# Attention and soft MoE on one core: key blocks of 128 within a batch, and value products over 128 rows

## The chip, the cores and the metric

The kernel runs on one core of a Trainium2 chip. The metric is device time in microseconds (us), from the first to the last instruction. An engine is named as in the profile: PE multiplies matrices (PEld loads its weights), DVE, ACT and POOL work on vectors, SP issues DMAs. [...]

## What is computed

Attention with one added to the denominator, over 8 batches, 12 heads, 448 positions and head size 64, and then a soft mixture of experts (32 slots, 8 experts) on the 3584 rows of 768.

```python
scores = scale * np.matmul(q, k.transpose(0, 1, 3, 2))
m = np.max(scores, axis=-1, keepdims=True)
e = np.exp(scores - m)
attn = e / (np.sum(e, axis=-1, keepdims=True) + np.exp(-m) + 1e-09)
x = np.matmul(attn, v)                       # then heads side by side: (3584, 768)
logits = x @ phi                             # softmax over rows gives slot inputs,
                                             # softmax over slots mixes the slot outputs
h = np.maximum(slot_input[e] @ w1[e], 0.0)   # per expert
slot_out[e] = h @ w2[e]
```

## The kernel before

**Units.** A unit u is two batches and two heads; 24 units run one after another, six (HP) to each pair of batches. A row of 448 positions is read as 64 partitions (P) of seven (TB) positions, so a tile has batch 0 in partitions 0 to 63 and batch 1 in 64 to 127, and seven blocks t of 64 positions per batch. C3 is 3: six of the seven query blocks are 128 wide, the seventh is 64 of each batch.

**Steps.** The program is a list of steps n, seven to a unit. In each step run, in this order, what the plan holds under "small", one score product (stage_S), what it holds under "mid" and "value", one transposed score product with its exp (stage_ST, 11 steps behind: LAG), and what it holds under "end" and "load". Every engine executes its instructions in the order in which this list issues them, and waits at the head of its queue. So a stage's place in a step is its place in every engine's queue.

**Stages of a unit that starts at step n = 7u.**
- load_qk (L114) and load_v (L120): q and k by DMA from POOL's queue with a cast to bf16, v by two DMAs from SP's queue in float32, after the cast of the v before it.
- stage_T (L194, step n - 1, mid): 28 transposes on PE into two banks; DVE copies the q half to SBUF (L204), ACT the k half (L205), behind it.
- stage_S (L208, steps n to n + 6): query x key scores, four products over a quarter of the array each; DVE reduces them to row maxima, a column of M (L219).
- stage_MT (L221, n + 7, small): PE transposes M, ACT copies it to mt (L225) and makes exp(-m), em (L227); POOL multiplies mt by a mask (L231, L237) into md.
- stage_ST (L242, n + 11 to n + 17): for key block t of 64 in both batches, ones x md subtracts the maximum and key x query adds the transposed scores; ACT writes exp of them to et (L256), four buffers.
- stage_V (L259, n + 10, load): POOL casts v to bf16 (L261) and sets a column of ones (L263).
- stage_AV (L266, steps n + AV0[t], mid): value products, et as weights; batch 0 over partitions 0 to 63 and batch 1 over 64 to 127, into a PSUM tile of two banks held from t = 0 until it is evacuated (16 products for each t).
- stage_AVout (L289, n + 19, value): ACT copies the tile to xu (L293) and xq (L296); xu is a single buffer.
- stage_shift (L300, n + 19, end): four small POOL copies bring the seventh block into place (L304); POOL adds em (L306) and 1e-9 (L307).
- stage_N (L310, n + 21, mid; n + 22, end, in units 1, 7, 13, 19): DVE's reciprocal (L313) and POOL's normalising product into x (L319).
- stage_X (L327, n + 27, value): PE transposes x, DVE copies it (L332).

After every sixth unit the mixture runs over the pair of batches, spread over the steps: logits, running maximum and sums over slots, gate softmax (L345 to L474). Weights come one load_w (L130) a unit on POOL's queue at step n + 7, "load", the rest after the last unit. Behind the steps come the experts' products and the output (L585 to L635).

**PSUM.** slot() (L94) hands out four buffers of two banks each, r0 to r3; each request takes the one that is due first by the LAGS table; the value products' buffer is out of the turn until release() (L101).

Of the kernel before, what the change touches and what calls it, by code (L numbers as in the profile page):

```python
# [9 lines left out]
F32 = mybir.dt.float32  # L10
# [6 lines left out]
P = 64  # L17
LAG = 11
AV0 = (15, 16, 16, 17, 18, 19, 19)
# [4 lines left out]
def kernel(  # L24
# [40 lines left out]
    for name, n, bufs in (("qr", N2, 1), ("kr", N2, 1), ("qk0", 2 * N2, 1), ("qk1", 2 * N2, 1),  # L65
                          ("vr", 2 * N2, 1), ("md0", N2, 1), ("v65", 2 * TB * 66, 1),
                          ("qk2", 2 * N2, 1), ("md1", N2, 1), ("v66", 2 * TB * 66, 1),
                          ("et", N2, 4), ("xu", 4 * TB * 65, 1), ("xq", 4 * 65, 1),
# [22 lines left out]
    LAGS = {"S": 3, "ST": 3.5, "T": 3, "X": 2.5, "M": 3, "held": 3.5}  # L91
    due, made, where = [0.0] * 4, [0], {}

    def slot(shape, dtype=F32, kind=None):  # L94
        made[0] += 1
        i = min(range(4), key=lambda j: (due[j], j))
        due[i] = made[0] + LAGS.get(kind, 2) if kind != "hold" else float("inf")
        where[kind] = i
        return psum.tile(shape, dtype, tag=f"r{i}", name="ps")

    def release():  # L101
        due[where["hold"]] = made[0] + LAGS["held"]

# [16 lines left out]
    def load_v(u):  # L120
        t_ = buf("vr", 0).bitcast(F32).rearrange("p (h n) -> p h n", h=2)
        RAW[u, "vr"] = load(u, t_, v, nc.sync if u else nc.gpsimd)
# [30 lines left out]
    ones = const.tile([128, P], BF16, name="ones")  # L153
# [8 lines left out]
    load_v(0)  # L162
    M = [const.tile([128, 128], BF16, name=f"m{i}") for i in range(2)]
# [27 lines left out]

    QT, KT, MD, ET, EM, AV, XU, X, DEN = {}, {}, {}, {}, {}, {}, {}, {}, {}

    def stage_T(u):  # L194
# [4 lines left out]
        for i, name in enumerate(("qr", "kr")):  # L199
            r = RAW.pop((u, name))  # L200
            for t in range(TB):
                for h in range(2):
                    nc.tensor.transpose(o[i][ds(h * D, D), :, ts(t, P)], r[:, h, ts(t, D)], ident)  # L203
# [4 lines left out]
    def stage_S(u, s):  # L208
        ps = slot([128, 2, 512], kind="S")
        for h in range(2):  # L210
            hs = ds(h * D, D)
            for r in range(2):

                b, o = divmod(s, C3) if s < 2 * C3 else (r, C3)
                o = o * 128 + (r * P if s < 2 * C3 else 0)
                nc.tensor.matmul(ps[ds(r * P, P), h, ds(0, S)], QT[u][hs, b, ds(o, P)],  # L216
# [4 lines left out]
    def stage_MT(u):  # L221
# [4 lines left out]
        em = small.tile([128, 2, TB], F32, tag="em", name="em")  # L226
# [15 lines left out]
    def stage_ST(u, t):  # L242
        ps = slot([128, 2, 512], kind="ST")
        for b in range(2):
            for h in range(2):
                hs = ds(h * D, D)
                nc.tensor.matmul(ps[ds(b * P, P), h, ds(0, S)], ones[hs, :], MD[u][hs, b, :],  # L247
                                 start=True, stop=False)
        for b in range(2):
            for h in range(2):  # L250
                hs = ds(h * D, D)
                nc.tensor.matmul(ps[ds(b * P, P), h, ds(0, S)],  # L252
                                 KT[u][hs, b, ds(t * P, P)], QT[u][hs, b, :],
# [5 lines left out]
    def stage_V(u):  # L259
# [3 lines left out]
        nc.gpsimd.memset(t_[:, :, :, ds(D, 1)], 1.0)  # L263
# [3 lines left out]

# [396 lines left out]
```

## Time and profile before

| what | value |
|---|---|
| runs | 356.85, 351.5, 354.83 us; median 354.83 |
| profiled execution | time and span 351.5 us |
| mean granted PE clock | 0.926 (1.00 in the main loop) |
| busy in the interval 69.64 to 79.49 us | PE 9.22, DVE 8.58, ACT 8.23, POOL 9.01 us |
| busy in 260.02 to 297.20 us (37.18 us) | PE 25.86, DVE 15.15, ACT 23.44, POOL 22.46 us |
| busy in 297.20 to 351.50 us (54.30 us) | PE 33.24, DVE 19.40, ACT 13.22, POOL 4.06 us |
| landing of a v load from SP | 3.2 to 10.6 us, median 7.2 |

The main loop runs from about 20 to 262 us; the last units, the experts and the output follow. A row of a timeline gives the start and the length of an instruction, or of several alike (xN), in us; in brackets stands how long its engine was idle ahead of it and which engine, tile and line ended that. Products on PE overlap, so their lengths do not add up; the distance between starts counts. Lengths on POOL are rough.

### The profile page before, as it was taken

The page shows a single profiled execution, that of the slowest core. Times are in us where ns is not written, and L with a number is a line of the kernel's source. Part 1 is how long each engine was busy: PE and PEld are TensorE (multiplying, and loading weights), DVE is VectorE, ACT ScalarE, POOL GpSimd, SP SyncE. Part 2 cuts the span into 40 slices and gives each one's busy share as a digit, 9 for nine tenths or more (in the row PEclk, how much of TensorE's full clock was granted, in tenths as well). Part 3 has the DMA queues.
Part 4 walks back from the last instruction along what each step waited for, and adds up shares of the span by engine and source line. Part 5 has one row for each costly group of instructions (what it writes and reads, how often), then busy time and mean ns, then how long its engine had stood idle before and what let it go on. Part 6 is the DMA issues. An engine that isn't in the chain of part 4 may idle for free.

```text
span 351.5 us, 14003 instructions
## 1 busy us (share of the span) xinstructions
PE 279.6 (80%) x6152; PEld 159.8 (45%) x6152; DVE 245.8 (70%) x321; ACT 223.1 (63%) x353; POOL 230.8 (66%) x413
## 2 busy tenths in 40 slices
PE   2679898998989789999968987899689745877760
PEld 1334554564555455556545544555455423342110
DVE  1886887988787978889888876878987015207440
ACT  1236887787778488888777776877588832015340
POOL 8335688899886878999876878698757573210000
PEclk9999999999999999999999999999999975596555
DMA  7455379789988898899997799869956599963997
GB/s 92 80 96 100 54 146 202 115 162 185 186 168 167 139 209 158 140 170 174 169 178 146 109 222 205 163 96 183 176 121 113 125 168 205 216 133 149 395 399 313
DMA packets 30061, 59.14 MB, mean 168 GB/s; under 512 B 4049, under 2 KB 22225, under 8 KB 30001
## 3 DMA queue, kind: packets, MB, share of 16 engines
q0 software_dynamic: 19344, 36.69, 61.7%
q1 hardware_dynamic: 10656, 21.57, 18.7%
q8 instruction: 48, 0.79, 0.9%
q14 instruction: 13, 0.10, 0.1%
HBM read 83.46 MB, written 11.01 MB: 269 GB/s over the span
## 4 chain that ended last, share of the span: by engine, by line
PE 31%; ACT 13%; DMA 12%; DVE 12%; issue 8%; POOL 6%; SPq 3%; ACTq 0%; POOLq 0%; DVEq 0%
PE ps L282 12%; ACT block L256 9%; PE ps L216 7%; DVE m L219 6%; PE ps L247 6%; DMA block<-in_moe_w_dram 5%; PE ps L252 4%; SPq L635 3%; DMA block<-in_v_dram 3%; DMA block<-in_k_dram 2%; DVE block L204 2%; DMA out_dram<-wres 2%; DVE sm L431 2%; ACT block L205 1%; POOL block L319 1%
## 5 line engine op out<-in xcount | busy, mean ns | idle before, releaser
L219 DVE TENSOR_REDUCE m<-ps 128x2 bf16<-128x896 f32 x168 | 179.5, 1090 | 41.4 <-PE ps L216 33.5
L256 ACT ACTIVATE block<-ps 128x896 bf16<-128x896 f32 x168 | 154.3, 922 | 49.9 <-PE ps L252 47.2
L216 PE MATMUL ps<-block 64*64 64x448 bf16 x672 | 66.6, 382 | 21.5 <-ACT block L205 12.0
L282 PE MATMUL ps<-block 64*128 64x65 bf16 (+1 forms) x2688 | 73.1, 196 | 4.2 <-issue 2.0
L282 PEld LDWEIGHTS <-block 64*128 64x128 bf16 (+1 forms) x2688 | 53.0, 97 | 42.6 <-issue 29.5
L247 PE MATMUL ps<-block,ones 64*64 64x448 bf16 x672 | 64.5, 364 | 5.4 <-ACT cT L445 2.4
L252 PE MATMUL ps<-block 64*64 64x448 bf16 x672 | 63.4, 356 | 0.0
L216 PEld LDWEIGHTS <-block 64*64 64x64 bf16 x672 | 32.3, 108 | 53.5 <-issue 37.4
L319 POOL TENSOR_TENSOR block<-block,rec 128x896 bf16<-128x896 f32 (+1 forms) x24 | 40.1, 1672 | 4.5 <-DVE rec L313 4.5
L304 POOL COPY block<-block 64x65 f32<-64x65 f32 x96 | 22.6, 236 | 26.5 <-ACT block L296 23.5
L231 POOL TENSOR_TENSOR block<-mt,nmask 128x768 bf16<-128x768 bf16 x24 | 36.0, 1502 | 3.9 <-ACT mt L225 2.7
L110 POOL DMA_DIRECT2D block<-in_q_dram x46 | 29.4, 640 | 14.0 <-PE ps L203 10.5
L205 ACT COPY block<-ps 128x896 bf16<-128x896 bf16 x24 | 21.8, 907 | 23.8 <-DVE block L204 23.8
L110 POOL DMA_DIRECT2D block<-in_k_dram x46 | 27.8, 618 | 2.0 <-issue 2.0
L247 PEld LDWEIGHTS <-ones 64*64 64x64 bf16 x672 | 23.5, 107 | 12.1 <-issue 7.4
L261 POOL CAST block<-block 128x896 bf16<-128x896 f32 x24 | 22.6, 941 | 5.8 <-DMA block<-in_v_dram 5.8
L203 PE MATMUL ps<-ident,block 128*64 128x128 bf16 x644 | 24.1, 228 | 2.0 <-DMA block<-in_q_dram 1.0
L203 PEld LDWEIGHTS <-block 128*64 128x64 bf16 x644 | 20.8, 115 | 8.2 <-issue 6.0
L252 PEld LDWEIGHTS <-block 64*64 64x64 bf16 x672 | 21.3, 109 | 0.9
L332 DVE COPY block<-ps 128x896 bf16<-128x896 bf16 x24 | 14.8, 616 | 9.7 <-PE ps L330 9.7
L293 ACT COPY block<-ps 128x780 f32<-128x780 f32 x24 | 19.5, 813 | 3.1 <-PE ps L282 2.0
L630 PE MATMUL ps<-wres,cT 32*128 32x384 bf16 x56 | 17.6, 493 | 4.5 <-DVE wres L633 2.5
(105 smaller groups left out, 254.4 us busy)
## 6 DMA issues: line engine op xcount, KB each, us to landing
wres<-in_moe_w_dram POOLq DMA_DIRECT2D x23, 768.0 KB, 7.7
out_dram<-wres SPq DMA_DIRECT2D x28, 384.0 KB, 4.2
block<-in_v_dram SPq DMA_DIRECT2D x46, 224.0 KB, 7.2
block<-in_moe_w_dram POOLq DMA_DIRECT2D x9, 768.0 KB, 12.8
block<-in_q_dram POOLq DMA_DIRECT2D x46, 112.0 KB, 4.8
block<-in_k_dram POOLq DMA_DIRECT2D x46, 112.0 KB, 4.5
block<-in_v_dram POOLq DMA_DIRECT2D x2, 224.0 KB, 4.2
wres<-in_q_dram POOLq DMA_DIRECT2D x2, 112.0 KB, 3.1
```

What stands on the lines that cost most here:

```text
L110: eng.dma_start(out=t_[ds(b * P, P), :, :], in_=src[bp * 2 + b, ds(hp * 2, 2)].rearrange("h (p t) d -> p h (t d)", t=TB))
L203: nc.tensor.transpose(o[i][ds(h * D, D), :, ts(t, P)], r[:, h, ts(t, D)], ident)
L205: nc.scalar.copy(t_[:, 1], o[1])
L216: nc.tensor.matmul(ps[ds(r * P, P), h, ds(0, S)], QT[u][hs, b, ds(o, P)], KT[u][hs, b, :], start=True, stop=True)
L219: nc.vector.tensor_reduce(m[:, :, s], ps[:, :, ds(0, S)], axis=AX.X, op=ALU.max)
L231: nc.gpsimd.tensor_tensor(md[:, :, ds(0, C3 * 128)].rearrange("p b (c n) -> p b c n", c=C3), mt.unsqueeze(1).unsqueeze(1).broadcast_to([12 ...
L247: nc.tensor.matmul(ps[ds(b * P, P), h, ds(0, S)], ones[hs, :], MD[u][hs, b, :], start=True, stop=False)
L252: nc.tensor.matmul(ps[ds(b * P, P), h, ds(0, S)], KT[u][hs, b, ds(t * P, P)], QT[u][hs, b, :], start=False, stop=True)
L256: nc.scalar.activation(et, ps[:, :, ds(0, S)], AF.Exp, scale=scale)
L261: nc.gpsimd.tensor_copy(t_[:, :, :, ds(0, D)], RAW.pop((u, "vr")).rearrange("p h (t d) -> p h t d", t=TB))
L282: nc.tensor.matmul(o, et[bs, h, ds(c * 128, w)], V65[u][bs, h, t, ds(0, 65)], start=(t == 0 and h == 0 and c == 0), stop=(t == TB - 1), sk ...
L319: eng.tensor_tensor(xo[:, hs], xv[:, hs, :, ds(0, D)], rec[:, hs].unsqueeze(3).broadcast_to([128, nh, TB, D]), op=ALU.mult)
```

## The change

Keys are put in another order by the k transposes (KPOS), so that 128 consecutive columns of K hold blocks c and c + 4 of one batch, and the last 64 hold block 3. v is loaded in the same order, by four DMAs in place of two. A key step then covers 128 keys of one batch (three steps for each batch) and one step 64 keys of both. The value products of a batch go over 128 rows into one bank of their own; batch 0 is evacuated at step n + 18, batch 1 at n + 21, by one ACT copy each. The shift moves to n + 21 and the normalising to n + 23 (n + 24 in units 1, 7, 13, 19), now in three POOL operations. Scores of a 128-wide query block are one product for each head in place of two. PSUM has three buffers of two banks and two of one bank, which also serve small tiles. em gets three buffers. The column of ones in v is set once at the start, on DVE. Three late weight loads move by one or two steps.

```diff
-AV0 = (15, 16, 16, 17, 18, 19, 19)
+AV0 = (15, 15, 17, 17, 19, 19, 20)
+AVO = (18, 21)
...
-    LAGS = {"S": 3, "ST": 3.5, "T": 3, "X": 2.5, "M": 3, "held": 3.5}
-    due, made, where = [0.0] * 4, [0], {}
+    LAGS = {"S": 3, "ST": 3.5, "T": 3, "X": 2.5, "M": 3}
+    due = {f"r{i}": 0.0 for i in range(3)} | {f"a{i}": 0.0 for i in range(2)}
+    made, held = [0], []
 
     def slot(shape, dtype=F32, kind=None):
         made[0] += 1
-        i = min(range(4), key=lambda j: (due[j], j))
-        due[i] = made[0] + LAGS.get(kind, 2) if kind != "hold" else float("inf")
-        where[kind] = i
-        return psum.tile(shape, dtype, tag=f"r{i}", name="ps")
+        one = mybir.dt.size(dtype) * shape[1] * (shape[2] if len(shape) > 2 else 1) <= 2048
+        small_ = [i for i in ("a0", "a1") if one and (kind == "AV" or due[i] <= made[0] + 1)]
+        i = min(small_ or ("r0", "r1", "r2"), key=lambda j: (due[j], j))
+        if kind == "AV":
+            assert due[i] < float("inf")
+            held.append(i)
+            due[i] = float("inf")
+        else:
+            due[i] = made[0] + LAGS.get(kind, 2)
+        return psum.tile(shape, dtype, tag=i, name="ps")
...
     def load_v(u):
         t_ = buf("vr", 0).bitcast(F32).rearrange("p (h n) -> p h n", h=2)
-        RAW[u, "vr"] = load(u, t_, v, nc.sync if u else nc.gpsimd)
+        bp, hp = divmod(u, HP)
+        for b in range(2):
+            src = v[bp * 2 + b, ds(hp * 2, 2)].rearrange("h (p t) d -> p h (t d)", t=TB)
+            for r, t0, t1, at_ in ((0, 0, C3 + 1 - b, b * (C3 + 1)), (1, C3 + 1 - b, TB, b * C3)):
+                (nc.sync if u else nc.gpsimd).dma_start(
+                    out=t_[ds(r * P, P), :, ds(at_ * D, (t1 - t0) * D)],
+                    in_=src[:, :, ds(t0 * D, (t1 - t0) * D)])
+        RAW[u, "vr"] = t_
...
+    for i in range(2):
+        nc.vector.memset(buf(f"v6{5 + i}", 0).rearrange("p (n e) -> p n e", e=66)[:, :, ds(D, 1)], 1.0)
...
+    KPOS = (0, 2, 4, 6, 1, 3, 5)
...
-                    nc.tensor.transpose(o[i][ds(h * D, D), :, ts(t, P)], r[:, h, ts(t, D)], ident)
+                    nc.tensor.transpose(o[i][ds(h * D, D), :, ts(KPOS[t] if i else t, P)],
+                                        r[:, h, ts(t, D)], ident)
...
-            for r in range(2):
-
-                b, o = divmod(s, C3) if s < 2 * C3 else (r, C3)
-                o = o * 128 + (r * P if s < 2 * C3 else 0)
-                nc.tensor.matmul(ps[ds(r * P, P), h, ds(0, S)], QT[u][hs, b, ds(o, P)],
+            if s < 2 * C3:
+                b, c = divmod(s, C3)
+                nc.tensor.matmul(ps[:, h, ds(0, S)], QT[u][hs, b, ts(c, 128)],
+                                 KT[u][hs, b, :], start=True, stop=True)
+                continue
...
     def stage_ST(u, t):
         ps = slot([128, 2, 512], kind="ST")
-        for b in range(2):
+        b, c = divmod(t, C3 + 1)
+        blocks = [(b, slice(0, 128), ts(c, 128))] if t != C3 else [
+            (b, ds(b * P, P), ds(C3 * 128, P)) for b in range(2)]
+        for b, rows, ks in blocks:
             for h in range(2):
                 hs = ds(h * D, D)
...
-        nc.gpsimd.memset(t_[:, :, :, ds(D, 1)], 1.0)
...
+            et = ET[u, t]
+            bs = (0, 1) if t == C3 else (t // (C3 + 1),)
+            if part == 0 and t in (0, C3):
+                AV[u, bs[-1]] = slot([128, 512], kind="AV")
             for h in range(2):
                 for c in (range(C3) if part == 0 else (C3,)):
-                    for b in range(2):
-                        bs = ds(b * P, P)
+                    for b in bs:
+                        av = AV[u, b]
+                        ks = ds(b * P, P) if t == C3 else slice(0, 128)
...
-                        nc.tensor.matmul(o, et[bs, h, ds(c * 128, w)],
-                                         V65[u][bs, h, t, ds(0, 65)],
+                        nc.tensor.matmul(o, et[ks, h, ds(c * 128, w)],
+                                         V65[u][ks, h, t, ds(0, 65)],
...
+    def stage_AVout(u, b):
+        xu = buf("xu", 0).bitcast(F32).rearrange("p (b n) -> p b n", b=2)
+        nc.scalar.copy(xu[:, b], AV.pop((u, b))[:, ds(0, TB * 65)])
+        XU[u] = xu.rearrange("p b (s e) -> p b s e", e=65)
         release()
 
     def stage_shift(u):
-        xu, xq = XU[u]
-        for h in range(2):
-            for b in range(2):
-                nc.gpsimd.tensor_copy(xu[ds(b * P, P), h, TB - 1, :], xq[ds(h * P, P), b, :])
+        xu = XU[u]
+        xq = buf("xq", 0).bitcast(F32)
+        R = 2 * C3
+        nc.gpsimd.tensor_copy(xq[ds(0, P)], xu[ds(P, P), 0, R])
+        nc.gpsimd.tensor_copy(xu[ds(P, P), 0, R], xu[ds(0, P), 1, R])
+        nc.gpsimd.tensor_copy(xu[ds(0, P), 1, R], xq[ds(0, P)])
         den = small.tile([128, 2, TB], F32, tag="den", name="den")
-        nc.gpsimd.tensor_tensor(den, xu[:, :, :, D], EM.pop(u), op=ALU.add)
+        em = EM.pop(u)
+        nc.gpsimd.tensor_tensor(
+            den[:, :, ds(0, R)].rearrange("p b (h c) -> p b h c", h=2),
+            xu[:, :, ds(0, R), D].rearrange("p b (h c) -> p b h c", h=2),
+            em[:, :, ds(0, R)].rearrange("p h (b c) -> p b h c", b=2), op=ALU.add)
+        nc.gpsimd.tensor_tensor(den[:, :, R], xu[:, :, R, D], em[:, :, R], op=ALU.add)
         nc.gpsimd.tensor_scalar(den, den, 1e-9, None, op0=ALU.add)
...
     def stage_N(u):
-        xv = XU.pop(u)[0]
+        xv = XU.pop(u)
+        R = 2 * C3
...
+        for b in range(2):
+            eng = nc.vector if b and u == U - 1 else nc.gpsimd
             eng.tensor_tensor(
...
+                x[:, ts(b, C3)].rearrange("p c (h d) -> p h c d", h=2),
+                xv[:, b, ds(0, R), ds(0, D)].rearrange("p (h c) d -> p h c d", h=2),
...
+        nc.gpsimd.tensor_tensor(
+            x[:, R].rearrange("p (h d) -> p h d", h=2), xv[:, :, R, ds(0, D)],
+            rec[:, :, R].unsqueeze(2).broadcast_to([128, 2, D]), op=ALU.mult)
...
-        at(n + 19, "value", lambda u=u: stage_AVout(u))
-        at(n + 19, "end", lambda u=u: stage_shift(u))
-
-        at(n + (22 if u % HP == 1 else 21), "end" if u % HP == 1 else "mid",
+        for b in range(2):
+            at(n + AVO[b], "value", lambda u=u, b=b: stage_AVout(u, b))
+        at(n + AVO[1], "end", lambda u=u: stage_shift(u))
+        at(n + AVO[1] + (3 if u % HP == 1 else 2), "end" if u % HP == 1 else "mid",
            lambda u=u: stage_N(u))
```

## The prediction

> **What bounds the kernel now.** I read the page's busy times first, then the stretches by stage, then the timeline of each engine over one period of the main loop, and the chain of waits last. The page shows four engines that are nearly equally loaded, so no share of busy time says which one counts:
>
> ```profile
> PE 279.6 (80%) x6152; PEld 159.8 (45%) x6152; DVE 245.8 (70%) x321; ACT 223.1 (63%) x353; POOL 230.8 (66%) x413
> ```
>
> The main loop makes one unit (two batches, two heads) per seven steps n; I call n mod 7 the phase. I cut it at the start of the copy of K (L205), which runs once per unit. The 20 intervals from 38.9 to 260.0 us last 9.85 us at best. Here is one of them, 69.64 to 79.49, on DVE, ACT, POOL and PE (timeline; columns: start, length, engine, line, operation):
>
> ```profile
> 68.99 0.61 DVE L204 COPY block<-ps 128x896 bf16<-128x896 bf16 x1
> ...
> 71.09 1.10 DVE L219 TENSOR_REDUCE m<-ps 128x2 bf16<-128x896 f32 x1 [0.96 <-PE ps L216]
> 72.10 0.23 DVE L313 RECIPROCAL rec<-den 128x14 f32<-128x14 f32 x1
> 72.25 6.69 DVE L219 TENSOR_REDUCE m<-ps 128x2 bf16<-128x896 f32 x6
> ```
>
> DVE never pauses except 0.96 us behind the K copy: seven maxima, two copies and a reciprocal are the interval. Delay one maximum and the interval grows by as much.
>
> ```profile
> 69.64 0.91 ACT L205 COPY block<-ps 128x896 bf16<-128x896 bf16 x1 [0.37 <-DVE block L204]
> ...
> 71.25 0.27 ACT L225 COPY mt<-ps 128x128 bf16<-128x128 bf16 x1
> ...
> 74.15 1.97 ACT L256 ACTIVATE block<-ps 128x896 bf16<-128x896 f32 x2 [0.31 <-PE ps L252]
> 76.44 0.92 ACT L256 ACTIVATE block<-ps 128x896 bf16<-128x896 f32 x1 [0.32 <-PE ps L252]
> 77.32 0.81 ACT L293 COPY block<-ps 128x780 f32<-128x780 f32 x1
> ...
> 79.49 0.91 ACT L205 COPY block<-ps 128x896 bf16<-128x896 bf16 x1 [0.37 <-DVE block L204]
> ```
>
> The exp of phase 4 starts at 76.44 (6.80 us into the interval) and ends at 77.36. The next line of PE that matters is the score product of phase 6:
>
> ```profile
> 68.81 0.56 PE L330 MATMUL ps<-ident,block 128*128 128x128 bf16 x7
> ...
> 74.21 0.51 PE L282 MATMUL ps<-block 64*128 64x65 bf16 x16
> 74.54 0.36 PE L247 MATMUL ps<-block,ones 64*64 64x448 bf16 x4
> ...
> 77.43 0.36 PE L216 MATMUL ps<-block 64*64 64x448 bf16 x4
> ```
>
> It starts 0.07 us after that exp: following slot() through the steps, the scores of phase 6 get the PSUM slot that the exp of phase 4 has just read. From the end of that exp to the next K copy are 79.49 - 77.36 = 2.13 us: product, last maximum, copy of Q, copy of K.
>
> ```profile
> 70.43 1.28 POOL L110 DMA_DIRECT2D block<-in_q_dram  x2 [0.21 <-issue]
> 71.70 1.21 POOL L110 DMA_DIRECT2D block<-in_k_dram  x2
> 72.89 1.51 POOL L231 TENSOR_TENSOR block<-mt,nmask 128x768 bf16<-128x768 bf16 x1
> 74.32 0.44 POOL L237 TENSOR_TENSOR block<-mt,nmask 128x128 bf16<-128x128 bf16 x1
> 74.68 1.72 POOL L319 TENSOR_TENSOR block<-block,rec 128x896 bf16<-128x896 f32 x1
> 76.31 0.62 POOL L141 DMA_DIRECT2D wres<-in_moe_w_dram  x1
> ...
> 78.36 1.06 POOL L304 COPY block<-block 64x65 f32<-64x65 f32 x4 [0.27 <-ACT block L296]
> 79.51 0.21 POOL L306 TENSOR_TENSOR den<-block,em 128x14 f32<-128x14 f32 x1
> 79.82 0.26 POOL L307 TENSOR_SCALAR den<-den 128x14 f32<-128x14 f32 x1
> ```
>
> POOL is full too, but its order suits the others: shift (phase 5), loads of Q and K, mask products, normalising (phase 0). L319 ends at 76.40 and ACT overwrites its input xu (L293) only at 77.32. That cover of 0.92 us is what the change touches.
>
> **The change, part by part.**
>
> *Scores and transposed scores (PE).* Six of seven steps lose half their products (12 and 24 per unit). A group of four quarter-array products takes 0.19 us (L247 at 73.49, L252 at 73.68), the time of its 448 columns; two half-array products have the same columns. I take 0; the bounds are 0 and +0.19 us per group if the two halves did not overlap (the pairs in L282 do).
>
> *Value products (PE).* 112 per unit become 48 over 128 rows and 16 over 64. 16 now take 0.33 us (74.21 to 74.54), 41 ns a pair; 56 pairs become 48 + 8 = 56 turns of the array. If a turn costs a pair, the change is 0, and I take that. Bounds: 65 columns at 448 per 0.19 us are 28 ns, 56 x (28 - 41) = -0.7 us per unit; the seven full-array transposes L330 take 0.51 us from 68.81 to the next group, 73 ns each, 48 x (73 - 41) = +1.5 us. Nearest is the pair, with the same 65 columns. One step with value products fewer saves one switch of array shape. [...]
>
> *Evacuation (ACT).* One copy of 780 (813 ns) and one of 130 (272 ns) become two of 455. The line through both rows, 0.83 ns an element, gives 543 ns each; back to back the old pair took 0.87 us (77.32 to 78.19), the new ones about 0.45 each. Cost 0 to +0.1. They move to phases 4 and 0, ahead of the exp there.
>
> *Shift (POOL).* Four copies at 0.265 become three; one add becomes two (0.31 each with its gap): 1.72 becomes 1.76 us. It moves from phase 5 to the end of phase 0, behind the mask products and past the loads of Q and K.
>
> *Normalising (POOL).* Rows 128x896 at 1704 ns and 128x448 at 956 give 1.67 ns an element: two of 384 and one of 128 are 0.77 + 0.77 + 0.34 = 1.88 us with overlapped issue, against 1.63 now. It moves from phase 0 to phase 2, behind the shift and the weight load (0.62). In units 1, 7, 13, 19 it comes one step later still. The memset L263 goes (0.16; two go to DVE at the start), off the path.
>
> *Loads of V (SP, DMA).* Two become four, of the same bytes in pieces of 768 and 1024 B. SP, otherwise idle here, takes about 0.6 us for each: +1.2. Landing is 7.2 us in the median, 10.6 at most; between one cast and the next lie 9.85 - 0.95 = 8.9 us. I take 0 while the interval is 11 us or more; bounds 0 and a landing twice as long if the four wait for each other.
>
> *PSUM.* The seven-step order of big slots stays: three of two banks for S, ST and T where four were shared with AV. The transposed maxima, X and the small tiles of the mixture use the two one-bank slots. 0, or a small gain where a score product had waited for the maxima's slot (interval 59.33 to 69.64: the first maximum waits 1.40 us).
>
> *What ends last then.* Time from the K copy: maxima copied on ACT at 1.88 (71.52). Loads of Q and K, now straight after PE's transposes (68.81), are issued by then. Mask products 1.93 to 3.72 (72.89 to 74.68 now is 1.79). Shift to 5.48. Weight load to 6.13. Normalising to 8.01. The reciprocal on DVE waits for the shift till 5.5, where the third maximum ends at about 4.9; the maxima queued behind it are 0.8 us late. But the evacuation of phase 4 overwrites xu, and must wait for all three parts of the normalising: 8.1. Behind it on ACT waits the exp: 8.55 to 9.47. Behind that the scores of phase 6, and 2.13 us later the K copy: **11.6 us** in place of 9.85. The 0.8 us are inside this, not added.
>
> The 14 intervals without mixture work sum to 145.7 us (9.84, 10.59, 10.31, 9.85, 10.78, 10.17, 10.82, 9.86, 9.85, 9.86, 10.82, 12.18, 9.87, 10.9); what lengthens some lies beside the new chain, so 14 x 11.6 = 162.4: +16.7. One has two weight loads: +0.6. Three with the gate's sums (13.6) normalise after the fourth maximum: 122.05 + 1.9, against an exp at 122.78 that now starts at 124.5: +1.7 each, +5.1. Three with logits (11.5 to 11.8): between 0 and 1.75, half of it: +2.6. At the end POOL's cast of unit 22 comes at 8.95 in place of 7.6 after the copy, then two more issues on SP, then 0.25 of normalising: +2.8. Sum +27.8 on the profiled execution's 351.5: **379**. That execution is the lowest of the three runs, whose median is 3.3 above; I say **380**.
>
> **Rivals.**
> 1. *The chain binds in part* (its rows on POOL are rough, and ACT comes later than reckoned). With 0.7 us an interval for 1.7, 351.5 + 20 x 0.7 + 2.8 = 368; with 0.2, 358. Against: every link is an in-order queue.
> 2. *Full-array products bind PE.* PE is busy 9.22 of 9.85 us; +1.5 and the 0.54 idle behind the K copy make 11.3. Alone: 14 x 11.3 - 145.7 + 6 x 1.45 = +21, 373; under the chain, nothing. [...]
> 3. *V late.* Four loads in a row on SP that wait for each other: 14 us to land, the cast pushes all POOL: 3 us an interval, 410. Partly so: 390 to 400. For: DMA engines are busy 0.91 of this interval. Against: only two waits for V now (5.8 us).
> 4. *Faster: fewer PE instructions.* 6152 products become about 4140. Four intervals hold a pause of about 0.9 us inside L282 with "issue" as its cause (86.35, 30 of 32 products, then 0.73 idle). Were these gone, and the waits on the maxima's slot, all 14 would be 9.85: -7.8, 344. It decides only if the normalising ends by 6.3 us into the interval, 1.7 before my sum: the shift would have to be ahead of the mask products on POOL, and its place in the step says it isn't.
>
> **How the numbers follow.** Chain as summed 0.56 (own range 369 to 391); in part 0.16; PE 0.08; V late 0.08; faster or no change 0.12. About 2% (7 us) is what a measurement of this kernel can tell from no change. Faster by more than that: 0.07, the better half of rival 4. Within it: 0.12, the rest of rival 4 and the lowest of rival 1. Slower: 0.81. The range 359 to 398 leaves out rival 4, and the worst of rival 3.
>
> **What would show it.** Right: intervals between K copies of 11.3 to 12 us; the evacuation of batch 0 on ACT idle till POOL's last normalising part; DVE idle ahead of the reciprocal, and ahead of the seventh maximum; the value products at about 41 ns a turn; POOL's order as listed. Wrong: intervals under 10.5 us, or ACT reaching that copy after POOL is done. A gap of PE between 128-row products would be rival 2; POOL's cast waiting for V rival 3.

## The result, and the profile after the change

| | before | after |
|---|---|---|
| median, us (before: all runs, those beside the new kernel too) | 354.6 | 396.63 (393.91 to 399.22) |
| ratio to before, 95% interval | | 1.122 [1.112, 1.132] |
| profiled span, us | 351.5 | 397.4 |
| regular interval between K copies, us | 9.85 | 11.90 |

The change made the kernel slower by 12%, and the chain that was predicted binds. The result is inside the predicted range (359 to 398), but at its upper end: the chain as summed had a range of 369 to 391 of its own, and 396.6 lies above it. Only the room that the range left for a late v takes it in. On the profiled executions the change costs 45.9 us where the sum said 27.8 (42.0 by the medians; the profiled execution after is the longest of its four). The part on why the prediction was right is about that difference. A span is 1.7 to 2.2 us less than the time wherever the record has both, so the kernel before's lowest time and its profiled execution, both 351.5, may be two executions. Single executions more than 1.5% above the fastest of the same kernel are left out of all ratios and of the medians of the experiments.

In the new kernel the K copy is L224, exp L279, evacuation L312, mask products L252 and L258, shift L320 to L330, reciprocal L337, normalising L341 and L346, POOL's cast of v L284, score products L233 and L237, maxima L240, transposed scores L271 and L276, value products L303. The page's first part and four of its groups of instructions:

```profile
PE 300.5 (76%) x4136; PEld 158.7 (40%) x4136; DVE 249.5 (63%) x323; ACT 220.7 (56%) x353; POOL 233.9 (59%) x438
...
L224 ACT COPY block<-ps 128x896 bf16<-128x896 bf16 x24 | 21.7, 905 | 44.2 <-DVE block L223 44.2
...
L341 POOL TENSOR_TENSOR block<-block,rec 128x384 bf16<-128x384 f32 x47 | 38.1, 836 | 5.6 <-DVE rec L337 5.3
L312 ACT COPY block<-ps 128x455 f32<-128x455 f32 x48 | 25.9, 543 | 21.0 <-POOL block L346 21.0
...
L337 DVE RECIPROCAL rec<-den 128x14 f32<-128x14 f32 x24 | 5.7, 238 | 23.6 <-POOL den L330 23.6
```

A third of PE's instructions are gone, and every engine but PE has almost the busy time it had; PE's rose from 279.6 to 300.5 us. What is new stands in the last column: ACT's evacuation waits 21.0 us for POOL's last normalising part (18 waits), DVE's reciprocal 23.6 us for the shift. Here is one regular interval, 76.88 to 88.78; first ACT and POOL in the timeline:

```profile
76.88 0.91 ACT L224 COPY block<-ps 128x896 bf16<-128x896 bf16 x1 [1.55 <-DVE block L223]
...
79.17 2.86 ACT L279 ACTIVATE block<-ps 128x896 bf16<-128x896 f32 x3
83.06 0.92 ACT L279 ACTIVATE block<-ps 128x896 bf16<-128x896 f32 x1 [1.04 <-PE ps L276]
85.07 0.54 ACT L312 COPY block<-ps 128x455 f32<-128x455 f32 x1 [1.09 <-POOL block L346]
85.50 1.73 ACT L279 ACTIVATE block<-ps 128x896 bf16<-128x896 f32 x2
88.78 0.91 ACT L224 COPY block<-ps 128x896 bf16<-128x896 bf16 x1 [1.54 <-DVE block L223]
```

```profile
78.85 1.46 POOL L252 TENSOR_TENSOR block<-mt,nmask 128x768 bf16<-128x768 bf16 x1 [0.32 <-ACT mt L246]
80.39 0.40 POOL L258 TENSOR_TENSOR block<-mt,nmask 128x128 bf16<-128x128 bf16 x1
80.85 0.23 POOL L320 COPY block<-block 64x65 f32<-64x65 f32 x1
...
82.09 0.25 POOL L330 TENSOR_SCALAR den<-den 128x14 f32<-128x14 f32 x1
82.40 0.64 POOL L156 DMA_DIRECT2D wres<-in_moe_w_dram  x1
83.06 1.63 POOL L341 TENSOR_TENSOR block<-block,rec 128x384 bf16<-128x384 f32 x2
84.63 0.40 POOL L346 TENSOR_TENSOR block<-block,rec 128x128 bf16<-128x128 f32 x1
```

POOL runs without a gap from the mask products (1.97 us after the K copy) to the end of the normalising (85.03, 8.15 after it). The evacuation starts 0.04 us later, after 1.09 us of idle time, and the exp queued behind it starts at 85.50. Then DVE and PE:

```profile
80.58 1.10 DVE L240 TENSOR_REDUCE m<-ps 128x2 bf16<-128x896 f32 x1 [0.17 <-PE ps L233]
82.37 0.24 DVE L337 RECIPROCAL rec<-den 128x14 f32<-128x14 f32 x1 [0.70 <-POOL den L330]
82.53 3.02 DVE L240 TENSOR_REDUCE m<-ps 128x2 bf16<-128x896 f32 x3
86.91 1.10 DVE L240 TENSOR_REDUCE m<-ps 128x2 bf16<-128x896 f32 x1 [1.36 <-PE ps L237]
```

```profile
78.96 0.72 PE L303 MATMUL ps<-block 128*128 128x65 bf16 x16
79.61 0.36 PE L271 MATMUL ps<-block,ones 64*128 64x448 bf16 x2
...
86.48 0.38 PE L237 MATMUL ps<-block 64*64 64x448 bf16 x4 [0.95 <-ACT block L279]
86.80 0.50 PE L303 MATMUL ps<-block 128*128 128x65 bf16 x8
87.13 0.95 PE L221 MATMUL ps<-ident,block 128*64 128x128 bf16 x28
```

The seventh score product starts at 86.48, as the first of the two exps ends (85.50 and 0.92 for one), and the last maximum waits 1.36 us for it. Sixteen 128-row value products take 79.61 - 78.96 = 0.65 us: 41 ns a turn, the pace of the pairs before.

### The profile page after: what moved, and what is told of

It is laid out like the page before. It is cut to its first block, busy times and chain, and to the rows that moved or that the text cites. A ratio compares the mean times of both kernels' runs of the same rounds, so it can differ in the third digit from the quotient of the medians.

```text
span 397.4 us, 10049 instructions
## 1 busy us (share of the span) xinstructions
PE 300.5 (76%) x4136; PEld 158.7 (40%) x4136; DVE 249.5 (63%) x323; ACT 220.7 (56%) x353; POOL 233.9 (59%) x438
## 3 DMA queue, kind: packets, MB, share of 16 engines
HBM read 83.46 MB, written 11.01 MB: 238 GB/s over the span
## 4 chain that ended last, share of the span: by engine, by line
POOL 26%; PE 20%; DMA 19%; ACT 11%; DVE 11%; issue 10%; SPq 1%; POOLq 0%; ACTq 0%; DVEq 0%
DMA block<-in_v_dram 9%; ACT block L279 8%; POOL block L341 5%; POOL block L252 5%; PE ps L303 5%; DMA block<-in_moe_w_dram 5%; PE ps L221 4%; DMA out_dram<-wres 4%; DVE m L240 4%; DVE block L223 3%; PE ps L271 2%; POOL block L118 2%; PE ps L233 2%; PE ps L237 2%; POOL wres L156 2%
## 5 line engine op out<-in xcount | busy, mean ns | idle before, releaser
L240 DVE TENSOR_REDUCE m<-ps 128x2 bf16<-128x896 f32 x168 | 178.9, 1090 | 67.4 <-PE ps L233 44.3
L279 ACT ACTIVATE block<-ps 128x896 bf16<-128x896 f32 x168 | 152.2, 924 | 58.8 <-PE ps L276 56.6
L233 PE MATMUL ps<-block 64*128 64x448 bf16 x288 | 57.3, 393 | 25.3 <-ACT block L279 9.3
L303 PE MATMUL ps<-block 128*128 128x65 bf16 (+3 forms) x1536 | 73.5, 203 | 3.8 <-POOL block L284 1.7
L271 PE MATMUL ps<-block,ones 64*128 64x448 bf16 (+1 forms) x384 | 65.5, 386 | 12.2 <-DVE m L240 10.6
L303 PEld LDWEIGHTS <-block 128*128 128x128 bf16 (+3 forms) x1536 | 54.8, 102 | 35.6 <-issue 22.1
L276 PE MATMUL ps<-block 64*128 64x448 bf16 (+1 forms) x384 | 64.0, 375 | 0.0
L233 PEld LDWEIGHTS <-block 64*128 64x128 bf16 x288 | 22.4, 99 | 70.1 <-issue 60.6
L224 ACT COPY block<-ps 128x896 bf16<-128x896 bf16 x24 | 21.7, 905 | 44.2 <-DVE block L223 44.2
L252 POOL TENSOR_TENSOR block<-mt,nmask 128x768 bf16<-128x768 bf16 x24 | 35.3, 1471 | 16.9 <-ACT mt L246 16.8
L341 POOL TENSOR_TENSOR block<-block,rec 128x384 bf16<-128x384 f32 x47 | 38.1, 836 | 5.6 <-DVE rec L337 5.3
L312 ACT COPY block<-ps 128x455 f32<-128x455 f32 x48 | 25.9, 543 | 21.0 <-POOL block L346 21.0
L271 PEld LDWEIGHTS <-ones 64*128 64x128 bf16 (+1 forms) x384 | 18.7, 98 | 35.7 <-DVE m L240 15.4
L284 POOL CAST block<-block 128x896 bf16<-128x896 f32 x24 | 22.3, 928 | 7.9 <-DMA block<-in_v_dram 7.9
L337 DVE RECIPROCAL rec<-den 128x14 f32<-128x14 f32 x24 | 5.7, 238 | 23.6 <-POOL den L330 23.6
L660 DVE COPY wres<-ps 128x768 f32<-128x768 f32 x14 | 13.4, 958 | 10.3 <-DMA out_dram<-wres 8.6
```

Of the source, the lines that this page charges most:

```text
L233: nc.tensor.matmul(ps[:, h, ds(0, S)], QT[u][hs, b, ts(c, 128)], KT[u][hs, b, :], start=True, stop=True)
L240: nc.vector.tensor_reduce(m[:, :, s], ps[:, :, ds(0, S)], axis=AX.X, op=ALU.max)
L252: nc.gpsimd.tensor_tensor(md[:, :, ds(0, C3 * 128)].rearrange("p b (c n) -> p b c n", c=C3), mt.unsqueeze(1).unsqueeze(1).broadcast_to([12 ...
L271: nc.tensor.matmul(ps[rows, h, ds(0, S)], ones[hs, ds(0, P * 2 // len(blocks))], MD[u][hs, b, :], start=True, stop=False)
L276: nc.tensor.matmul(ps[rows, h, ds(0, S)], KT[u][hs, b, ks], QT[u][hs, b, :], start=False, stop=True)
L279: nc.scalar.activation(et, ps[:, :, ds(0, S)], AF.Exp, scale=scale)
```

## The experiments

Ratios are to the kernel before, in runs made together with it. "Interval" is the regular distance between K copies in the profiled execution. A forecast's total is a time, to be held against the median.

| run | made from | median, us | ratio [95%] | span, us | interval, us |
|---|---|---|---|---|---|
| e1_xu2 | after | 386.2 | 1.086 [1.077, 1.095] | 381.2 | 10.89 |
| e2_order | after | 400.5 | 1.127 [1.119, 1.134] | 399.9 | 12.13 |
| e4_vr2 | after | 396.2 | 1.114 [1.106, 1.122] | 394.7 | 11.90 |
| e8_xu2_order_vr2 | after | 369.2 | 1.037 [1.031, 1.043] | 367.8 | 10.89 |
| e10_spread | e8 | 360.7 | 1.013 [1.007, 1.019] | 356.5 | 10.50 |
| e3_oldplace | after | 371.6 | 1.047 [1.040, 1.053] | 368.7 | 10.16 |
| e6_old_vr2 | e3 | 360.9 | 1.014 [1.008, 1.019] | 359.3 | 10.16 |
| e5_moved | before | 373.3 | 1.047 [1.039, 1.054] | 374.2 | 10.46 |
| e5b_moved | before | 358.8 | 1.011 [1.007, 1.016] | 356.1 | 10.46 |
| e9_v4 | before | 367.5 | 1.032 [1.025, 1.039] | 364.7 | 9.85 |
| e11_tsep | e6 | 353.6 | 0.996 [0.993, 0.999] | 351.3 | 10.45 |
| e12_tsep_x | e11 | 347.3 | 0.981 [0.975, 0.987] | 345.5 | 9.94 |

### Is it the single xu buffer? e1_xu2

```diff
-        xu = buf("xu", 0).bitcast(F32).rearrange("p (b n) -> p b n", b=2)
+        xu = wres[:, WRES - 1, ds(0, 4 * TB * 65)] if u % 2 and u < 20 else buf("xu", 0)
+        xu = xu.bitcast(F32).rearrange("p (b n) -> p b n", b=2)
```

> The changed kernel with a second buffer for xu (units with odd numbers up to 19), nothing else. Theory (the evacuation of batch 0 on ACT waits for the normalising on POOL): that wait goes, the interval between K copies falls from 11.9 us to what DVE's wait for the shift leaves, about 9.85 + 0.85 = 10.7 us, in some 16 intervals; total 397 - 19 = 375 to 382 us. Rival (128-row value products or the three two-bank PSUM buffers hold the loop): no change, 393 to 399. Rival (v in four pieces, two landings one behind the other): no change, or POOL's cast now waits for v and the interval stays above 11.

Measured: interval 10.89, the ratio down from 1.122 to 1.086. ACT's timeline, 71.98 being a K copy:

```profile
78.16 0.92 ACT L279 ACTIVATE block<-ps 128x896 bf16<-128x896 f32 x1 [1.04 <-PE ps L276]
78.98 0.53 ACT L313 COPY block<-ps 128x455 f32<-128x455 f32 x1
79.39 0.94 ACT L279 ACTIVATE block<-ps 128x896 bf16<-128x896 f32 x1
```

The evacuation follows the exp without a pause, and the interval loses 1.01 us: the predicted wait was the end of the chain. The total misses its forecast (386.2 for 375 to 382). In the profiled execution one interval is 17.15 us, with a POOL cast waiting 5.4 us for v, and the next 14.11. DVE's reciprocal still waits 0.71 us for the shift there (77.48), and I took that for what holds 10.89.

### The shift ahead of the mask products: e2_order, then e8_xu2_order_vr2

```diff
         EM[u] = em
+        MT[u] = mt
+
+    def stage_MD(u):
+        mt = MT.pop(u)
...
         at(n + 7, "small", lambda u=u: stage_MT(u))
+        at(n + 7, "end", lambda u=u: stage_MD(u))
```

The mask products, now a stage of their own, stand in POOL's queue behind the shift of two units before.

> The changed kernel with POOL's mask products issued behind the shift instead of ahead of it. Theory (xu's wait binds, DVE's wait for the reciprocal lies inside it): the reciprocal no longer waits, but the normalising ends no earlier, since the same operations lie ahead of it and the shift waits for the evacuation of batch 1 at 2.4 us: interval 12.2 us, total 397 to 405. Rival (DVE's wait for the shift binds): 0.85 us less in 20 intervals, 380. Rival (PE or PSUM): no change, 393 to 399.

As expected: the reciprocal does not wait, but the normalising comes no sooner, the evacuation waits 27.1 us for it in place of 21.0, and the interval is 12.13. In e8 the same edit stands with the second xu buffer, and with a second buffer for raw v (e4's edit, below).

> The changed kernel, its places kept, with the three waits taken away: a second buffer for xu, a second buffer for raw v (both for odd units up to 19), and the mask products issued behind the shift so that DVE's reciprocal does not wait. Theory: the interval falls from 11.9 to 10.0 to 10.4 us; the units from 20 on, with single buffers, stay slow; total 358 to 368. If each of the two waits could hold the loop alone, the second buffer of xu (10.9) and the order (12.1) show it only together. Rival (PE or PSUM): 378 or more.

The forecast was missed (interval 10.0 to 10.4, total 358 to 368). The interval did not move from 10.89, though the wait on the reciprocal was gone from it (in DVE's timeline it starts at 78.50, with no idle time ahead). So that wait had cost nothing, and my reading of e1 was wrong. PE's timeline, 73.80 being a K copy, shows what ends last:

```profile
78.15 0.36 PE L236 MATMUL ps<-block 64*128 64x448 bf16 x2 [0.22 <-ACT block L286]
78.45 0.95 PE L310 MATMUL ps<-block 128*128 128x65 bf16 x24
79.33 0.36 PE L278 MATMUL ps<-block,ones 64*128 64x448 bf16 x2
...
80.95 0.36 PE L236 MATMUL ps<-block 64*128 64x448 bf16 x2 [0.50 <-ACT block L286]
81.25 0.72 PE L310 MATMUL ps<-block 128*128 128x65 bf16 x16
```

The score product of phase 3 waits for an exp to free its PSUM slot (PSUM holds the tiles `ps`, which PE writes). Behind it stand 24 value products (0.88 us), then the transposed scores and their exp (79.98), then the next score product at 80.95, 7.15 us after the K copy, again behind an exp. In e1 it is 79.13 - 71.98 = 7.15 too.

The span fell by 13.4 us even so. The two late intervals that were 17.15 and 14.11 in e1 are 10.90 and 11.66, and the three with the gate's sums are 12.4 where they were 14.5 to 15.8. In those, one DVE instruction had taken 2.38 us while POOL ran its mask product; here the product comes later, and it takes 0.24 (last section).

### The value products spread as before: e10_spread

```diff
-AV0 = (15, 15, 17, 17, 19, 19, 20)
+AV0 = (15, 16, 16, 17, 18, 19, 19)
```

> The run e8_xu2_order_vr2 with the value products spread over steps as before (AV0 = 15, 16, 16, 17, 18, 19, 19). Theory (the 10.9 us left in e8 come from PE, where the value products of two key steps stand in one step ahead of the transposed scores): the interval falls to 10.1 to 10.4, total 355 to 361. Rival (the evacuation in phase 0 and 4 on ACT is what holds 10.9): no change, 367 to 371.

10.50 (0.1 above the forecast) and a total of 360.7: the lumped value products ahead of the transposed scores cost 0.4 us an interval. The span falls by 11.3, of which 6.4 lie in the 14 ordinary intervals, the rest ahead of them, in those with mixture work and behind the last.

### All places as before the change: e3_oldplace, e6_old_vr2

```diff
-AV0 = (15, 15, 17, 17, 19, 19, 20)
-AVO = (18, 21)
+AV0 = (15, 16, 16, 17, 18, 19, 19)
+AVO = (19, 19)
...
-        at(n + AVO[1] + (3 if u % HP == 1 else 2), "end" if u % HP == 1 else "mid",
+        at(n + (22 if u % HP == 1 else 21), "end" if u % HP == 1 else "mid",
```

> The changed kernel with the places of before: value products in steps 15 to 19, both evacuations at 19, shift at 19, normalising at 21 or 22. Key blocks of 128, products over 128 rows, five PSUM buffers and four v loads stay. Theory (the cost is the place on POOL's and ACT's queues): intervals of 9.9 to 10.3 us, total 350 to 362, where two landings of v one behind the other (about 9 us) may just hold POOL's cast. Rivals (PE, PSUM): still 380 or more. Rival (v): POOL's cast waits in most units, 370 or more.

The interval fell to 10.16, but the total by less than expected, which spoke for the rival on v. The waits of POOL:

```profile
POOL block L284 <- DMA block<-in_v_dram: 27.3, 9, 7.8
```

Nine casts wait for v, 27.3 us in all. e6 adds the second raw buffer of v, loaded a unit earlier:

```diff
+        t_ = wres[:, WRES - 2, ds(0, 2 * N2)] if u % 2 and u < 20 else buf("vr", 0)
...
+        if u + 2 < 21:
+            at(n + 10, "load", lambda u=u: load_v(u + 2))
```

> The changed kernel with the places of before and a second buffer for raw v (odd units up to 19). Theory (what was left of the loss with the old places was v's four loads, which land in two turns): POOL's cast no longer waits, intervals of 10.0 to 10.2 us, total 352 to 360. Rival (128-row products and three PSUM buffers cost as well): 364 or more.

Between the two forecasts. By the medians, e3 is 16.9 us over before, and 10.7 of them were the loads of v (371.6 to 360.9). The rest does not lie in the ordinary intervals, although the regular one is 10.16 against 9.85: the 14 sum to 145.5 us in e6 and to 145.7 before, where several were longer than regular. Of the 7.8 us that e6's span has more, 3.5 are in the three intervals with the gate's sums, 1.4 in those with logits, 1.1 ahead of the fourth K copy and 2.0 behind the last. With its stages in their old places the changed tiling costs 1.4%, and with e3's loads of v 4.7%. The places cost most of the 12%: 1.122 against 1.047 with one buffer for v, 1.114 (e4, below) against 1.014 with two.

### The loads of v alone: e9_v4, e4_vr2

e9 is the kernel before, with its two loads of v cut in four:

```diff
-        RAW[u, "vr"] = load(u, t_, v, nc.sync if u else nc.gpsimd)
...
+        for t0, t1 in ((0, C3 + 1), (C3 + 1, TB)):
+            for b in range(2):
+                src = v[bp * 2 + b, ds(hp * 2, 2)].rearrange("h (p t) d -> p h (t d)", t=TB)
+                (nc.sync if u else nc.gpsimd).dma_start(
+                    out=t_[ds(b * P, P), :, ds(t0 * D, (t1 - t0) * D)],
+                    in_=src[:, :, ds(t0 * D, (t1 - t0) * D)])
...
```

> The kernel before with the load of v cut into four pieces of the same bytes, the second two waiting for the first two as in the changed kernel. Theory: landing takes about 9 us where the loop leaves 8.9, so POOL's cast waits in part of the units, 5 us in the worst: total 356 to 370, and about the loss that the changed kernel with the places of before shows (1.047) if v is all that is left there. Rival (v's pieces hidden): 351 to 356.

```profile
POOL block L268 <- DMA block<-in_v_dram: 35.2, 15, 7.6
```

3.2% for two more DMAs. Regular intervals stay at 9.85; two grow to 15.44 and 15.56. Why the loads are late is in the chain of waits, here that of the kernel after (in e9's own, 6.55 us of landing from 45.76 and 7.03 from 52.96 stand one behind the other):

```profile
85.93 0.60 SPq L134
86.53 0.04 issue
86.57 5.33 DMA block<-in_v_dram
91.92 2.85 DMA block<-in_v_dram
```

Pieces three and four write the tile that one and two write, and their landing begins only when those have landed: 8.2 us in two landings in a row.

> The changed kernel with a second buffer for raw v (odd units up to 19), so that v is loaded one unit earlier. Theory: the intervals of 11.9 us stay; only the one or two units in which POOL's cast waited for v (5 us) and what came behind it go: 386 to 394. Rival (v's landing holds the loop): 360 or less.

In the kernel after, the second buffer gained next to nothing (ratios 1.114 and 1.122, intervals overlapping), and 396.2 misses the 386 to 394 forecast: an interval of 11.9 us already hides most landings (in the kernel after two of 24 casts wait for v, 7.9 us in all). The cast that waited 5.00 us is gone, and with it one long interval (14.89, now 11.90). The other one stays (15.28, now 15.00), so v wasn't its cause: in both kernels POOL pauses 2.3 us between its two loads of q there, with "issue" named, which I leave open.

### The shift and the normalising moved, and nothing else: e5_moved, e5b_moved

```diff
-        at(n + 19, "end", lambda u=u: stage_shift(u))
+        at(n + 21, "end", lambda u=u: stage_shift(u))
...
-        at(n + (22 if u % HP == 1 else 21), "end" if u % HP == 1 else "mid",
+        at(n + (24 if u % HP == 1 else 23), "end" if u % HP == 1 else "mid",
```

em gets three buffers, as in the change.

> The kernel before with one thing of the change: the shift at step n + 21 (end) and the normalising at n + 23 (24 in units 1, 7, 13, 19), em in three buffers. Products, PSUM, v loads and the evacuation at n + 19 are those of before. Theory (the place on the queues costs): the reciprocal on DVE waits for the shift until 5.5 us behind the K copy, 0.85 late; the normalising ends at 7.9, and the evacuation, one step later here than in the changed kernel, waits for it about 0.3 us; intervals of 10.6 to 11.0 us in place of 9.85, total 368 to 378. Rival (products, PSUM or v loads are what costs): no change, 351 to 358.

e5 in this form lets a late weight load overwrite the last unit's xu before its normalising reads it, so that unit's rows of x are others, and PE waits 19.2 us for that normalising at the end. Its total is therefore no answer; e5b moves that load two steps.

> The run e5_moved again, with the late weight load that overlies xu two steps later (end + 17), so that the last unit's normalising no longer waits for it: the kernel before with the shift at n + 21 and the normalising at n + 23. Theory: the intervals of e5_moved (10.46 us in place of 9.85) and a tail like before's, total 362 to 367. Rival (place costs nothing): 351 to 358.

358.8, just above the rival's 351 to 358 and under the 362 forecast: a regular interval of 10.46, 0.6 more than before. The reciprocal waits 26.4 us in all, yet the total grows by 1.1% only. Fourteen times 0.61 would be 8.5, and the ordinary intervals grow by 5.5, since some were longer before; the third interval even shrinks (9.85 here against 11.46). So the move is cheap while both evacuations stay at n + 19. In the change batch 0's comes a step earlier, and for that one the late normalising isn't done: e1 has the price.

### Can the changed tiling win? e11_tsep, e12_tsep_x

In both kernels ACT's K copy follows DVE's Q copy (44.2 us of idle time in the page after). Both read one two-bank PSUM tile. e11 takes e6 and gives each half a bank of its own:

```diff
-        ps = slot([128, 2, 1024], BF16, "T")
+        pt = [slot([128, 1, 1024], BF16, "T") for _ in range(2)]
...
```

> The run e6_old_vr2 with the transposes of q and k in a PSUM tile of one bank each, so that ACT's copy of K waits for PE alone and not for DVE's copy of Q. Theory (the 0.96 us in which DVE idles behind the K copy are part of every interval): 0.3 to 0.6 us less in each of 23 intervals, total 347 to 354, at or under the kernel before. Rival (PE or the PSUM turn holds the interval at 10.16): 358 to 362.

The total fell to that of before, as forecast, though not for the reason given: the regular interval rose to 10.45. DVE's timeline says why: the transposes of x now got the tile whose Q copy had just begun. What fell are the three intervals with the gate's sums, by 7.8 of the 8.0 us of span (15.18, 15.11 and 13.92 in e6; 12.33, 12.04 and 12.05 here).

```profile
77.83 0.61 DVE L225 COPY block<-ps 128x896 bf16<-128x896 bf16 x1
79.08 0.62 DVE L361 COPY block<-ps 128x896 bf16<-128x896 bf16 x1 [0.64 <-PE ps L359]
```

e12 raises T in the table LAGS from 3 to 4.5, so that they get another tile.

> The run e11_tsep with a longer due time for the transposes' PSUM tiles (LAGS T = 4.5), so that the transposes of x take another tile and no longer wait on PE for DVE's copy of Q (0.82 us ahead of everything else on PE in e11). Theory: the first scores of a unit start about 0.8 us earlier, intervals of 9.5 to 9.8 us in place of 10.45, total 340 to 348, under the kernel before. Rival (something else holds 10.45, the PSUM turn with one big tile fewer): 351 to 356.

```profile
86.75 0.61 DVE L225 COPY block<-ps 128x896 bf16<-128x896 bf16 x1
87.00 0.91 ACT L226 COPY block<-ps 128x896 bf16<-128x896 bf16 x1 [0.24 <-PE ps L223]
87.50 0.62 DVE L361 COPY block<-ps 128x896 bf16<-128x896 bf16 x1
...
111.72 0.17 DVE L460 TENSOR_SCALAR sm<-sm 128x8 f32<-128x8 f32 x1
```

The 0.64 us are gone, the K copy runs beside the Q copy, and the interval is 9.94, above the 9.5 to 9.8 forecast. The total, 347.3, is in its forecast, and with a ratio of 0.981 [0.975, 0.987] this version beats both kernels; whether by a full 2% is open. Its gain over before lies in the gate's intervals (11.60, 11.31 and 11.32 us against 13.64, 13.53 and 13.53) and not in the regular ones. These are 2.0 to 2.2 us shorter each, and the `TENSOR_SCALAR` in each took 2.23 to 2.41 us before and takes 0.17 here, where POOL's mask product starts 1.1 to 1.3 us behind it in place of 0.7 to 0.9 (last section). So the gain is about what this one instruction had lost beside POOL. That the tiling itself gains anything is not shown, and no run moved the two apart in the kernel before.

## Why the prediction was right, and where its sum was short

**The chain.** Up to the evacuation the times came within 0.15 us. In microseconds from the K copy, predicted and measured: mask products 1.93, 1.97; shift done 5.48, 5.46; normalising done 8.01, 8.15; evacuation 8.1, 8.19; next K copy 11.6, 11.90. In one place luck helped: the shift began at 3.97 for 3.72 and took 1.49 for 1.76. e1 shows that the evacuation's wait on xu ended it: without it, 10.89. That the reciprocal's delay lies inside was right too (e2, and e1 against e8). But xu's wait is only 1.01 of the 2.05 us by which the interval grew. The sum charged all of it to the chain, as if 9.85 lay below; the steps back are 10.50 with the value products spread (e10), 10.16 with all places as before (e6), and 9.85.

**The sum.** By kind of interval, in us added on the profiled executions:

| part | predicted | measured |
|---|---|---|
| up to the first K copy, and three intervals of the start | 0 | 2.1 |
| 14 ordinary intervals | 17.3 | 30.9 |
| three with logits | 2.6 | 2.1 |
| three with the gate's sums | 5.1 | 6.2 |
| from the last K copy on | 2.8 | 4.7 |
| sum | 27.8 | 45.9 |

The term that fell short most is "14 x 11.6": it made every ordinary interval regular. The 14 came out 13.6 us above their forecast.

- Ten are regular, at 11.90 or a little more: +3.2. Of the 0.3 that I left out, 0.23 lie behind the exp: from its end to the K copy are 2.36 us for 2.13, because eight value products now stand between the seventh score product and the transposes (0.33 us, 86.80 to 87.13), and the Q copy, at 88.12, waits for the transposes.
- Two that follow the gate's last work are 13.77 and 13.38: +4.0. I had written that "what lengthens some lies beside the new chain". It lies ahead of it: PE stops there behind ACT's copies of the gate, and the first maximum waits 2.42 us (143.37) where it waits 0.93 in a regular interval, so the chain on POOL starts 0.9 us late. That is not all. In the first of the two the evacuation does not even wait for POOL, and PE's granted clock is 0.50 from 143.0 to 146.5; in the second it waits 0.24 us. e1, with a clock of 1.00 there and no wait on xu, has 12.36 and 12.35.

```profile
142.75 0.22 PE L244 MATMUL ps<-ident,m 128*128 128x128 bf16 x1 [1.48 <-ACT cT L472]
...
150.32 0.53 ACT L312 COPY block<-ps 128x455 f32<-128x455 f32 x1
```

- Two are 14.89 and 15.28: +7.0. In the first POOL's cast waits for v, then the whole queue behind it is late. (The three shares add up to 14.2: the 0.6 that the sum had set apart for the second weight load is in the 13.38.)

```profile
244.25 0.93 POOL L284 CAST block<-block 128x896 bf16<-128x896 f32 x1 [5.00 <-DMA block<-in_v_dram]
...
247.55 1.51 POOL L252 TENSOR_TENSOR block<-mt,nmask 128x768 bf16<-128x768 bf16 x1
```

Rival 3 thus came true in one interval of 14, and e4 confirms it (11.90 there). The cause of the 15.28 stays open. My bound "a landing twice as long" was the right end to keep, and zero the wrong value to take for every unit: I reasoned from the median landing, where the late unit decides. e9 prices the same edit at 3.2% on the kernel before.

**A stall costs twice.** In that interval PE waits for a maximum, and what follows runs at another pace; PE's timeline, and the stretches of the regular and the disturbed interval (columns: length, then busy time of PE, PEld, DVE, ACT, POOL, the granted clock, DMA share, GB/s):

```profile
252.38 0.56 PE L271 MATMUL ps<-block,ones 64*128 64x448 bf16 x2 [2.96 <-DVE m L240]
252.73 0.58 PE L276 MATMUL ps<-block 64*128 64x448 bf16 x2
...
253.61 1.10 PE L303 MATMUL ps<-block 128*128 128x65 bf16 x16
254.64 0.55 PE L271 MATMUL ps<-block,ones 64*128 64x448 bf16 x2
```

```profile
76.88:88.78 11.90, 9.79 (x152) 5.37 (x148) 8.63 (x11) 8.09 (x12) 9.05 (x18) 1.00 0.82 145
242.99:257.88 14.89, 11.01 (x152) 5.68 (x148) 8.73 (x11) 8.16 (x12) 10.61 (x19) 0.89 0.70 131
```

After 2.96 us of idle time a group takes 0.35 us in place of 0.20, and sixteen value products 1.03 in place of 0.65. The granted clock is 0.50 from about 252.3 to 255.7 us, and 0.89 over the stretch. The sum held no such term. The clock went to 0.50 within the pauses of 2.96 us (at 252.28) and of 2.46 us (at 265.94), and 0.3 us behind one of 1.48 us (at 143.06), while the same 1.48 us in e1 (ending at 135.02) and 2.13 us in the kernel before (ending at 118.96) left it at 1.00. So the length of one pause doesn't decide it; what does, no run shows.

This is part of PE's 300.5 us of busy time with a third fewer products: the four disturbed ordinary intervals have 11.01 to 12.12 us of it, the regular one 9.79. But the regular one, at full clock, is above before's 9.22 too. An estimate from the rows: PE pauses five times in it, before once, and at each pause the last 0.16 us of a group (0.36 long, 0.20 from start to start) no longer lie under the next group; four times that is 0.6.

**The other terms.** Score products by halves cost next to nothing, as taken: groups follow at 0.19 to 0.20 us as before, but where transposed scores stand right behind a score product it is 0.29 (80.17 to 80.46) for 0.19 (70.59 to 70.78). Rival 2 is refuted: value products keep 41 ns a turn in the mean. Twelve weight loads of 128*128 from 78.95 take 0.42 us together, 29 ns from start to start, though one lasts 98 ns in the median; then 0.12 us pass between the starts where the shape changes to 128*64 (79.30 to 79.42), as they did before the change from 64*128 to 64*64 (74.37 to 74.49). Rival 4's gain from fewer instructions was not seen under the chain: the pauses inside the value products that it named are gone (four before, none in PE's waits after), and the interval did not feel it. Rival 1 did not happen: in a regular interval the chain binds in full. The gate's three intervals came near their forecast (5.1 and 6.2), but not by its reason alone: the evacuation waits only 0.19 to 0.67 us for POOL in them, and the granted clock is 0.89 where it was 1.00; without the wait on xu (e1) they are 15.79, 14.53 and 14.52 against 15.57, 15.49 and 15.82. The sum had nothing for the start, which became 2.1 us longer, most of it in the second and third interval (10.48 and 12.39 for 9.65 and 11.46); no run tried it by itself. The tail's further 1.9 us contain a wait of 2.88 us for v in POOL's cast at 324.38; no run tried it by itself.

**What I had not seen.** Below the chain lay a second bound, PE's own order (e8 to e10, 0.4 us an interval), for which the sum had no term; the wait on xu covered it. The 0.34 us left between e10 and e6 I did not settle: the evacuations on ACT ahead of two exps are a candidate that no run tried alone.

## What to carry to other kernels

When a stage is moved, list every in-order queue it is moved past and time the first thing behind it that reuses its buffer; here one buffer, read by POOL a step too late, ended the chain and cost 1.0 us in each regular interval. The forecast of where the chain ends was sound; what lies below it was not asked. Then do not multiply the regular interval: intervals that are already disturbed, and the one unit whose load is late, held more of what the sum missed than the regular ones' error, and a stall of 3 us was paid again in PE's pace. When a version wins, see in which intervals: e11 and e12 drew level with the kernel before and passed it in the gate's, by about what one DVE instruction had lost there, and not in the regular ones that they were built for. A second buffer shows whether a wait was the bound, and the next bound must be read anew, for the wait that remains in the list may cost nothing (e1, e8).

## What the runs showed of the hardware

- Two engines' copies out of one two-bank PSUM tile ran one after the other in these kernels, and side by side from two tiles. With one tile the K copy began 0.03 to 0.21 us behind the end of the Q copy in all 24 units of the kernel before, and 0.03 to 0.04 in the kernel after. With two, in e12, it began 0.25 us behind the start of a Q copy of 0.61 us (86.75 and 87.00); in e11 its waits were for PE's transposes (15.9 us, 10 times). Whether the hardware or the program's recorded order sets this, no run here tells.
- One `TENSOR_SCALAR` of 128x8 on DVE, in the gate's sums, took 2.38 us where its neighbour of 128x1 took 0.14, and ended 0.05 us behind POOL's mask product (128.76 to 130.27). Over all runs it took 2.2 to 2.4 us wherever it began 0.65 to 0.87 us ahead of that product (26 times in nine kernels, the kernel before among them), and each time ended 0.03 to 0.05 us behind it. Where it began 1.08 us or more ahead it took 0.17 to 0.25 (e2, e8, e10, e11, e12), but for one case (e9: 1.39 ahead, 1.48 us). Behind the last unit, with no mask product near, it always took 0.17. What makes it wait, no run shows.

```profile
125.62 0.14 DVE L409 TENSOR_SCALAR stat<-nm 128x1 f32<-128x1 f32 x1
...
127.94 2.38 DVE L458 TENSOR_SCALAR sm<-sm 128x8 f32<-128x8 f32 x1
```

- Cutting 2 DMAs of a load into 4 of which the second two wait for the first made the kernel before 3.2% slower, with the same bytes (e9).
